# Early row maxima of a two-layer FNet and MQA kernel: one at a time, behind any matmul slot where a build-time estimate has a PSUM bank free

## The chip, the cores and the metric

One NeuronCore of one Trainium2 chip runs the whole program. The metric is the device time of one execution in microseconds (us). The kernel before was timed three times; the number to be predicted is the same time for the changed kernel.

The engines are named as the profile names them: PE is TensorE's matrix array (PEld its weight loads), DVE VectorE, ACT ScalarE, POOL GpSimd, SP SyncE, which issues most DMAs. PE writes its results into PSUM banks, from which DVE and ACT read them.

## The reference

Two layers, each an FNet mixing sublayer (A) and a multi-query attention sublayer (B), with S = 2048 rows, D = 512, H = 32 heads of 16:

```python
def _A_ref(x, ...):                       # FNet: y = Real(DFT_seq(DFT_hidden(x)))
    a = einsum("bsd,ed->bse", x, dft_hid_re); b = einsum("bsd,ed->bse", x, dft_hid_im)
    return einsum("ts,bse->bte", dft_seq_re, a) - einsum("ts,bse->bte", dft_seq_im, b)
def _B_ref(x, wq, wk, wv, wo):            # one k and one v for all 32 heads
    q = (x @ wq) ...; k = x @ wk; v = x @ wv
    scores = einsum("bhqd,bkd->bhqk", q, k) * Dh ** -0.5
    return einsum("bhqk,bkd->bhqd", softmax(scores), v) ... @ wo
x = A_x
for _ in range(2):
    x = x + _A_ref(_layernorm(x), ...)
    x = x + _B_ref(_layernorm(x), ...)
```

Products that need float32 accuracy are made of three products of a high and a low part (`mm3`: high times high, high times low, low times high).

## The kernel before

**Phases.** Each layer has a phase A (`phase_a`) and a phase B (`phase_b`). Phase A is a loop over 128 steps n. The steps stand in four blocks tb of 32 (one block makes 512 output rows); in a block the first 16 steps add up the real part and the next 16 the imaginary part of z = (layer-normed x) times the DFT matrix of the sequence, one 128-row chunk of the sum per step. After step 31, 63 and 95 (and in two parts at the end) the block's four row tiles are multiplied by the DFT matrix of the hidden axis (y), added to x, normalised, transposed (`tr_tile`), and multiplied into k and v (`kv`) and q (`q_mm`) during the first eleven steps of the next block; q is stored in DRAM (`qd`) and loaded back for one row tile i at a time (`qT_load`, 1 MB, a DMA on SP's queue). Phase B has 512 steps of scores, exponentials (ACT) and products with v.

**Row halves.** From step ROWS = 48 on, z (`z_rows`, L691) and y (`y_rows`, L494) use matmuls on half of PE's rows: each slot is a pair, one matmul on rows 0 to 63 (g = 0) and one on rows 64 to 127 (g = 1), which run side by side. A z step is 12 such pairs.

**Early maxima.** Softmax needs the maximum of each query row over the 2048 keys, for 16 row tiles i, 16 head pairs pr and two heads g. Each maximum is over four key quarters kb of 512. One matmul of a row half gives the 128 x 512 scores of one head and one quarter in one PSUM bank, and DVE reduces them (L381). Phase B makes most of them, up to three per step (`more_max`); a part is made early, in phase A from step 48 on. The table EARLY lists these: (i, quarter, slot for q, step of its `qT_load`, first time, last time). The times count 40 units per block, 32 for the steps and 8 for y. Quarter "f" means quarters 0 and 1 in one pass (`max_two`): two matmuls against the difference of the keys (L389, `kd`), their Relu on ACT (L394, tiles `rel` for g = 0 and `kraw` for g = 1), two matmuls against quarter 1, and one DVE instruction per g that adds and takes the maximum (L392). So one head pair of an "f" entry issues four matmuls in a row, and one of another entry two.

The order of all instructions is written out by this code at build time, and each engine runs its own in that order. Between z's pairs the early maxima stand at fixed places: `phase_a` spreads the 16 head pairs of an entry evenly between its two times, on quarters of a step (`inner`). They use three PSUM banks tagged "y", and one tagged "z"; the transposes also use "z", and `kv` and `q_mm` use "y". A matmul into a bank waits until DVE or ACT has read what the bank held, and since PE takes its matmuls in order, what stands behind it waits too.

Per layer EARLY has 8 entries of 32 plain maxima (256 matmuls) and 5 "f" entries of 64 matmuls (320), 576 in all.

Of the kernel before, what the change touches and what calls it, by code (L numbers as in the profile page):

```python
# [47 lines left out]
def fnet_mqa_kernel(ctx: ExitStack, tc: tile.TileContext, x_in, ct, dt_, wq, wkv, wo, out):  # L48
# [139 lines left out]
    def make_layer(L, src, mid, dst, last):  # L188
# [23 lines left out]
        def c_split(n):  # L212
            if n < 128:
                hls[n] = hl_tiles()
                split_sb(raws[n // 2][:, n % 2, :], *hls[n], None if L == 0 and n < 20 else nc.gpsimd)
# [36 lines left out]
        def tr_tile(t, x, xth, xtl, raw=None):  # L252
            pt = bank("z")
            for k in range(NK):
                nc.tensor.transpose(pt[:, k * P:(k + 1) * P], x[:, k * P:(k + 1) * P], ident)
            v = [ap.rearrange("p (a b) -> p a b", a=NK) for ap in (pt, raw or pt)]
            if raw:
                split_act(v[0], xth, xtl, v[1])
            else:
                split_ps(v[0], xth, xtl)  # L260

        def kv(t0, n, xth, xtl, vt=None, now=True):
            pk = bank("y")[:, :n * P]
            for k in range(NK):
# [11 lines left out]
        def kv_lo(t0, n):  # L276
            cs = slice(t0 * P, (t0 + n) * P)
# [4 lines left out]
        def k_diff(tb):  # L282
            if tb == 0:
# [17 lines left out]
        def q_mm(tb, g, xth, xtl):  # L301
            wh, wl = st["wqh", g]
            pq = bank("y")
            for k in range(NK):
# [63 lines left out]
        def partial(i):  # L368
            if i not in o.mxp:
                o.mxp[i] = sb.tile([P, NPAIR, 2, 4 if i else 5], F32, name=f"mxp{i % 4}")  # L370
                for e, (i_, kb, *_) in enumerate(KEPT):
                    for k in (0, 1) if kb == "f" else (kb,):
                        if i == i_:
                            nc.gpsimd.tensor_copy(o.mxp[i][:, :, :, k], st["mxe"][:, e])
# [8 lines left out]
        def max_two(i, pr, to):  # L383
            rows = [sb.tile([P, 512], F32, name=m) for m in ("rel", "kraw")]
            for k, c in ((st["kd"], 0), (kz, 512)):
                pm = [bank("z" if c and g else "y") for g in range(2)]
                for g in range(2):
                    gs = slice(64 * g, 64 * g + KR)
                    nc.tensor.matmul(pm[g], o.qT[i][gs, pr, :], k[gs, c:c + 512], start=True, stop=True)  # L389
                for g in range(2):  # L390
                    if c:
                        nc.vector.tensor_tensor_reduce(rows[g], pm[g], rows[g], 1.0, -3.0e38, ALU.add, ALU.max, to[:, g:g + 1])  # L392
                    else:
                        nc.scalar.activation(rows[g], pm[g], AF.Relu)  # L394

        def max_early(e, pr, at):
            i, kb = EARLY[e][:2]
            free = at < 80
            if "mxe" not in st:
                st["mxe"] = sb.tile([P, len(KEPT), NPAIR, 2], F32, name="mxe")  # L400
            if kb == "f":
                max_two(i, pr, st["mxe"][:, KEPT.index(EARLY[e]), pr] if i else partial(0)[:, pr, :, 0])
                if i == 0 and pr == NPAIR - 1:
                    nc.gpsimd.tensor_copy(partial(0)[:, :, :, 1], partial(0)[:, :, :, 0])
                return
            for g in range(2):
                to = st["mxe"][:, KEPT.index(EARLY[e]), pr, g:g + 1] if i else partial(0)[:, pr, g, kb:kb + 1]
                max_of(i, pr, g, kb * 512, 512, to, "z" if pr % 2 and g and free else "y")
# [66 lines left out]
        def y_out(t, y, x1):  # L475
            nc.vector.tensor_add(x1, y, x1)  # L476
# [6 lines left out]
        def y_rows(tb, pairs, zh, zl, x1, after):  # L483
            ys = [pair() for _ in pairs]
            at = 0
            for h in range(2):
                for w, y in zip(pairs, ys):
                    for cc, k in [(c, k) for c in range(2) for k in range(NK)][::1 - 2 * h]:
                        for u in (0, 1, 2)[::1 - 2 * h]:
                            a, b = ((zh, dh), (zh, dl), (zl, dh))[u]  # L490
                            for g in range(2):
# [3 lines left out]
                                                 start=(h, cc, k, u) == (0, 0, 0, 0), stop=(h, cc, k, u) == (1, 0, 0, 0))  # L495
                        for fn in after.get(at, ()):
# [78 lines left out]
        def prep_tasks(tb, x1):  # L575
# [15 lines left out]
            def ap(j):  # L591
                return lambda: ln_apply(x1[j], x1[j], 4 * tb + j)
# [21 lines left out]
        def phase_a(extra):  # L614
# [22 lines left out]
            for e, (i, kb, k, n0, n1, n2) in enumerate(EARLY):  # L637
                if n0 is not None:
                    add(n0, lambda i=i, k=k: qT_load(i, k))
                for pr in range(NPAIR):  # L640
                    u = n1 + pr * (n2 - n1) / NPAIR
                    at = divmod(int(4 * u), 4)
                    b, n = divmod(at[0], 40)
                    at = (32 * b + n, at[1]) if n < 32 else ("y", b, 4 * (n - 32) + at[1])
                    inner.setdefault(at, []).append(lambda e=e, pr=pr, u=u: max_early(e, pr, u))
# [26 lines left out]
            def z_split(z, hi, lo, c, d, late=False):  # L672
                if d % 2 == 0:
                    return
                if c or late:
                    for e in (d - 1, d):
# [5 lines left out]
            def z_rows(z, odd, chunks, first, last, split):  # L682
                order = [(j, u) for j in range(len(chunks)) for u in range(3)]
                for q in range(NK):
                    for e, (j, u) in enumerate(order[::-1] if q > 1 else order):
                        s, ch, cl = chunks[j]
                        a, b = ((xnh, ch), (xnh, cl), (xnl, ch))[u]
                        for g in range(2):
# [3 lines left out]
                                             start=first and q < 2 and e == 0, stop=last and q > 1 and e == len(order) - 1)  # L692
                        if 2 * e + 2 == len(order):
# [7 lines left out]
            def z_split_half(z, h, d):  # L701
                for e in (d - 1, d):
# [31 lines left out]
            for n in range(128):  # L734
# [12 lines left out]
                if n in (26, 58, 90, 114):  # L747
                    for tt in range(4):
                        x1[tt] = half(tt)
                        nc.sync.dma_start(x1[tt], src[4 * tb + tt])  # L750
# [376 lines left out]
```

## Time and profile before

| what | value |
|---|---|
| three runs | 3713.89, 3715.13 (median), 3718.11 us |
| the profiled execution: its own time; span of its instructions | 3717.63 us; 3715.8 us |
| granted TensorE clock, mean | 0.989 |
| busy: PE, DVE, ACT, POOL | 3607.8, 2644.9, 2533.2, 889.4 us |
| layer 0: first row-half matmul of z; last of them before y of block 3 | 203.3 us; 639 us |
| layer 1: the same two | 2048.3 us; 2478.8 us |
| phase B's exponentials are set up (ACT table load) in layer 0; in layer 1 | 717.8 us; 2557.7 us |

How to read it: times in the rows of a profile are us from the start of the span, those of one instruction in ns in the views that group. Matmuls are pipelined, and a matmul that starts every 0.23 us is shown as 0.39 us long, so that "busy" PE overlaps itself; how fast PE works is read from the starts, not from the busy share. A bracket at a row's end is the idle time before it and what ended it. The two layers run the same phase A program, so a stretch of one can be laid beside the same stretch of the other.

### The profile page before, as it was taken

What the parts mean: (1) busy time and instruction counts of PE and PEld (TensorE: products, weight loads), DVE (VectorE), ACT (ScalarE), POOL (GpSimd) and SP (SyncE); (2) the same over time, 40 slices, a digit from 0 to 9 for tenths busy, and PEclk for the clock granted to TensorE, in tenths of its full rate; (3) what the DMA queues carried; (4) which work ended last, traced back from release to release, by engine and by line L of the source; (5) the groups of instructions that cost most, each with busy time, mean ns of one, the idle gap of its engine ahead of it and who ended that gap; (6) DMA issues with size and microseconds to landing.
All of it is one profiled execution on the core that took longest, in us unless ns stands there. A gap on an engine that the chain in (4) does not pass through costs nothing.

```text
span 3715.8 us, 64466 instructions
## 1 busy us (share of the span) xinstructions
PE 3607.8 (97%) x24672; PEld 1866.1 (50%) x24672; DVE 2644.9 (71%) x4845; ACT 2533.2 (68%) x3278; POOL 889.4 (24%) x1270
## 2 busy tenths in 40 slices
PE   8999999999999999999999989999999999999999
PEld 6776667633333333333378756675333333333333
DVE  6155665588888888888411756666888888888882
ACT  3223544388888888888933245344888888888888
POOL 5543232112212211221254323231111011011101
PEclk9999999999999999999999999999999999999999
DMA  6544223311111110110134342324111111001101
GB/s 189 155 138 129 79 91 111 111 42 36 48 33 36 40 32 24 33 47 25 41 125 118 126 137 69 107 82 120 36 45 35 36 37 47 24 22 47 35 22 27
DMA packets 224389, 254.56 MB, mean 69 GB/s; under 512 B 52368, under 2 KB 174288, under 8 KB 216912
## 3 DMA queue, kind: packets, MB, share of 16 engines
q1 hardware_dynamic: 210384, 233.12, 20.8%
q0 software_dynamic: 13696, 17.33, 1.8%
q8 instruction: 194, 3.18, 0.4%
q14 instruction: 115, 0.94, 0.1%
HBM read 184.02 MB, written 65.27 MB: 67 GB/s over the span
## 4 chain that ended last, share of the span: by engine, by line
PE 85%; DVE 5%; ACT 4%; issue 3%; DMA 2%; POOL 1%; SPq 0%; ACTq 0%; POOLq 0%; DVEq 0%
PE z L866 27%; PE x L852 18%; PE y L380 14%; PE x L691 9%; PE x L494 2%; PE y L87 2%; PE y L88 2%; PE y L89 2%; PE x L89 2%; PE x L87 2%; PE x L88 2%; DVE mxe L381 1%; PE y L389 1%; ACT rel L394 1%; DVE kraw L392 1%
## 5 line engine op out<-in xcount | busy, mean ns | idle before, releaser
L855 ACT ACTIVATE slot<-x 128x1024 f32<-128x1024 f32 x1990 | 1938.3, 1025 | 297.1 <-PE x L852 282.6
L381 DVE TENSOR_REDUCE mxp<-y 128x1 f32<-128x512 f32 (+1 forms) x3040 | 1894.3, 678 | 219.5 <-PE y L380 205.4
L866 PE MATMUL z<-slot,v 128*32 128x512 f32 x8192 | 1098.9, 606 | 1.5 <-DVE lnv L977 0.7
L380 PE MATMUL y<-kz,slot 64*128 64x512 f32 (+1 forms) x2678 | 742.6, 401 | 27.8 <-DVE mxe L381 8.6
L852 PE MATMUL x<-slot,kz 64*128 64x512 f32 x2956 | 679.3, 453 | 6.6 <-DMA slot<-mt 4.3
L852 PEld LDWEIGHTS x<-slot,kz 64*128 64x128 f32 x2956 | 279.7, 185 | 749.5 <-ACT slot L855 674.7
L380 PEld LDWEIGHTS y<-kz,slot 64*128 64x128 f32 x2678 | 355.9, 188 | 100.0 <-DVE mxe L381 24.7
L79 POOL TENSOR_TENSOR cl<-craw,ch 128x512 fp32r<-128x512 f32 x236 | 302.3, 1298 | 334.9 <-ACT ch L78 271.2
L691 PE MATMUL x<-ch,xnh 64*128 64x512 f32 (+1 forms) x1536 | 338.6, 367 | 8.2 <-DVE row L476 6.2
L866 PEld LDWEIGHTS z<-slot,v 128*32 128x32 f32 x8192 | 164.4, 108 | 361.0 <-issue 330.6
L691 PE MATMUL x<-ch,xnl 64*128 64x512 f32 (+1 forms) x1536 | 337.9, 366 | 0.3
L381 DVE TENSOR_REDUCE mxe<-y 128x1 f32<-128x512 f32 x406 | 259.2, 684 | 110.9 <-PE y L380 86.0
L691 PE MATMUL x<-cl,xnh 64*128 64x512 f32 (+1 forms) x1536 | 336.2, 359 | 0.0
L448 POOL DMA_DIRECT2D slot<-mt x208 | 102.8, 502 | 615.9 <-PE y L380 559.4
L78 ACT CAST ch<-craw 128x512 fp32r<-128x512 f32 x256 | 152.6, 620 | 119.2 <-PE x L691 53.4
L392 DVE CUSTOM_DVE_ANT_0 rel<-y,rel 128x512 f32<-128x512 f32 x160 | 110.7, 692 | 171.4 <-ACT rel L394 133.2
L691 PEld LDWEIGHTS x<-ch,xnh 64*128 64x128 f32 x1536 | 192.8, 189 | 35.4 <-DVE row L476 7.7
L691 PEld LDWEIGHTS x<-cl,xnh 64*128 64x128 f32 x1536 | 200.4, 189 | 19.8
L907 POOL TENSOR_TENSOR row<-row,row 128x256 f32<-128x256 f32 x63 | 46.4, 737 | 680.0 <-DMA row<-rd 657.3
L691 PEld LDWEIGHTS x<-ch,xnl 64*128 64x128 f32 x1536 | 194.9, 189 | 23.2 <-issue 4.5
L394 ACT ACTIVATE rel<-y 128x512 f32<-128x512 f32 x160 | 95.4, 596 | 116.8 <-PE y L389 94.7
L87 PE MATMUL x<-ch,xnh 128*128 128x512 f32 x384 | 155.9, 406 | 14.7 <-ACT ch L78 11.5
(186 smaller groups left out, 3934.5 us busy)
## 6 DMA issues: line engine op xcount, KB each, us to landing
craw<-ct_in SPq DMA_DIRECT2D x112, 512.0 KB
slot<-qd SPq DMA_DIRECT2D x44, 1024.0 KB
qd<-row SPq DMA_DIRECT2D x144, 128.0 KB
od<-row SPq DMA_DIRECT2D x252, 64.0 KB
row<-wqd SPq DMA_DIRECT2D x48, 256.0 KB
row<-x_in SPq DMA_DIRECT2D x32, 256.0 KB
mid<-row POOLq DMA_DIRECT2D x32, 256.0 KB, 2.3
craw<-ct_in SPq DMA_DIRECT2D x32, 256.0 KB
```

What stands on the lines that cost most here:

```text
L78: nc.scalar.copy(hi, raw)
L79: (eng or nc.vector).tensor_sub(lo, raw, f(hi))
L87: nc.tensor.matmul(ps_, ah, bh, start=start, stop=False)
L88: nc.tensor.matmul(ps_, ah, bl, start=False, stop=False)
L89: nc.tensor.matmul(ps_, al, bh, start=False, stop=stop)
L380: nc.tensor.matmul(pm, o.qT[i][gs, pr, :], kz[gs, c0:c0 + n], start=True, stop=True)
L381: nc.vector.reduce_max(to, pm, axis=AX.X)
L392: nc.vector.tensor_tensor_reduce(rows[g], pm[g], rows[g], 1.0, -3.0e38, ALU.add, ALU.max, to[:, g:g + 1])
L691: nc.tensor.matmul(z[d], a[gs, s, d * P:(d + 1) * P], b[gs, :], start=first and q < 2 and e == 0, stop=last and q > 1 and e == len(order) - 1)
L852: nc.tensor.matmul(st["e"][:, g, :], kz[64 * g:64 * g + KR, c * P:(c + 1) * P], o.qT[i][64 * g:64 * g + KR, cp:cp + 4, :], start=True, sto ...
L855: nc.scalar.activation(ptiles[i, s_][:, 2 * w:2 * w + 2, :], st.pop("e"), AF.Exp, scale=DH ** -0.5)
L866: nc.tensor.matmul(a[32 * j:32 * j + 32, :], v1[:, c, :], pt[:, j, :], start=c == 0, stop=c == NT - 1)
```

## The change

1. The fixed places go. Every entry of EARLY becomes a list of single matmuls (`work`): head pair, part ("u" a plain maximum; "d" the difference and "b" quarter 1 of an "f" entry), g. After each pair of z (`z_rows`) and of y (`y_rows`) the code calls `pump`, which emits at most one of them: of the entries whose first step has come, the one with the earliest last step, if its next single is on the right row half and if the estimate has a bank free.
2. The estimate (`clk`) is kept while the program is written: `spend` adds fixed costs for the work that is emitted, `serve` gives DVE 0.6 and ACT 0.5 us for each item, and `held` notes until when a bank is taken, whichever of the four is free first. `flush` emits without regard to it what an entry still has left when its last step comes.
3. A single matmul on one row half shifts the halves by one slot: from there each pair of z and y is emitted with g = 1 first (`order`, `st["skew"]`), until the next single, so that the halves still take turns.
4. EARLY has other entries, steps (now counted in n) and loads. The "f" entry of row tile 0 becomes two plain ones, (2, 2) goes, and (1, 2) comes for 8 head pairs. Per layer that is 304 plain maxima and 4 "f" entries (256 matmuls), 560 in all; `units` gives phase B the other 16. There are as many `qT_load` as before, at steps 44, 44, 45, 64, 77, 77, 84, 96, 96, 101, 107 where they were at 44, 44, 50, 66, 66, 78, 78, 95, 97, 101, 107.
5. In phase B the shifts of row tile 14 are gathered in two halves of 8 head pairs, as those of tile 15 were, which adds 16 small DMAs per layer, 8 on SP's queue and 8 on POOL's.

```diff
 EARLY = [
-    (1, 0, 2, 44, 56, 63.5), (2, 0, 3, 44, 63.5, 70.9), (3, 0, 8, 50, 70.9, 86.5),
-    (0, "f", 0, 66, 88, 95), (1, 1, 1, 66, 87, 95), (3, 1, 8, None, 88.25, 112),
-    (4, "f", 2, 78, 95.5, 103), (5, "f", 3, 78, 103, 110.9), (6, "f", 8, 95, 115.5, 122.5),
-    (2, 1, 0, 97, 122.5, 128), (2, 2, 0, None, 128, 133.9), (7, "f", 2, 107, 136, 143), (0, 2, 8, 101, 134.5, 148.5),
+    (1, 0, 2, 44, 48, 63, 16), (2, 0, 3, 44, 48, 63, 16), (3, 0, 8, 45, 48, 66, 16), (0, 0, 0, 64, 66.5, 79, 16),
+    (0, 1, 0, None, 71.5, 79, 16), (3, 1, 8, None, 71.5, 84, 16), (4, "f", 2, 77, 79.5, 95, 16), (5, "f", 3, 77, 79.5, 95, 16),
+    (6, "f", 8, 84, 87, 128, 16), (2, 1, 0, 96, 98, 111, 16), (1, 1, 1, 96, 98, 111, 16), (1, 2, 1, None, 103.5, 111, 8),
+    (7, "f", 2, 107, 109.5, 119, 16), (0, 2, 8, 101, 103.5, 128, 16),
 ]
...
-        def max_two(i, pr, to):
...
-        def max_early(e, pr, at):
...
+        clk = {"pe": 0.0, "dve": 0.0, "act": 0.0, "y": [0.0] * 3, "z": 0.0}
+        def spend(pe=0.0, dve=0.0, act=0.0):
+            clk["pe"] += pe
+            for k, v in (("dve", dve), ("act", act)):
+                if v:
+                    clk[k] = max(clk[k], clk["pe"]) + v
+        def serve(eng, ready):
+            clk[eng] = max(clk[eng], ready) + (0.6 if eng == "dve" else 0.5)
+            return clk[eng] + 0.2
...
+        def pump(n, only=None):
+            for e in sorted((e for e in work if work[e] and EARLY[e][4] <= n), key=lambda e: EARLY[e][5]):
+                if only in (None, e) and work[e][0][2] == st["skew"] and issue(e, *work[e][0], only is not None):
+                    work[e].pop(0)
+                    st["skew"] ^= 1
+                    return True
+            return False
+        def issue(e, pr, part, g, force):
...
+            tag = "z" if clk["z"] <= clk["y"][0] else "y"
+            free = clk["z"] if tag == "z" else clk["y"][0]
+            if part == "b":
+                free = max(free, st["rel"][g][1] - 0.7)
+            elif part == "d" and g in st["rel"]:
+                return False
+            if free > clk["pe"] + 0.05 and not force:
+                return False
...
+            pm = bank(tag)
+            nc.tensor.matmul(pm, o.qT[i][gs, pr, :], k[gs, c0:c0 + 512], start=True, stop=True)
+            ready = max(clk["pe"], free) + 0.5
...
+                end = serve("dve", ready)
+            held(tag, end)
+            clk["pe"] += 0.116
+            return True
+        def flush(n):
+            for e in work:
+                while work[e] and EARLY[e][5] <= n:
+                    if not pump(n, e):
+                        assert any(pump(n, k) for k in work if work[k])
+                    clk["pe"] = max(clk["pe"], clk["dve"] - 1.0)
+        def order(*x):
+            return x[::-1] if st["skew"] else x
...
-                        for g in range(2):
+                        for g in order(0, 1):
                             d = ((0, 2, 1, 3), (1, 3, 0, 2))[g ^ odd][q]
...
+                        spend(pe=0.231 if len(chunks) == 2 else 0.116)
+                        pump(st["n"])
...
-                for at, j, p0, np_ in (..., (NSTEP - AHEAD, i + 1, 0, HALF if i == NT - 2 else NPAIR)):
-                    if j in (0, NT - 1) or j == i + 1 < NT:
+                for at, j, p0, np_ in (..., (NSTEP - AHEAD, i + 1, 0, HALF if i >= NT - 3 else NPAIR)):
+                    if j in (0, NT - 2, NT - 1) or j == i + 1 < NT:
```

What this does to the order on PE is seen at two places of layer 0. The first is step 72, just behind block 1's q products (L87 to L89). `slot` is a q tile, `kd` the difference of the keys, `x` a bank of z, `y` and `z` the four banks of the maxima; x2 is a pair. Before:

```order
L691 MATMUL x<-ch,xnh 128x512 x2
L691 MATMUL x<-cl,xnh 128x512 x2
L691 MATMUL x<-ch,xnl 128x512 x2
L389 MATMUL y<-kd,slot_2758 128x512 x2
L389 MATMUL y<-kz,slot_2758 128x512
L389 MATMUL z<-kz,slot_2758 128x512
L380 MATMUL y<-kz,slot_2760 128x512 x2
L691 MATMUL x<-ch,xnh 128x512 x2
L691 MATMUL x<-cl,xnh 128x512 x2
L691 MATMUL x<-ch,xnl 128x512 x2
```

And now, from the same pair of z:

```order
L749 MATMUL x<-ch,xnh 128x512 x2
L440 MATMUL y<-kz,slot_2703 128x512
L749 MATMUL x<-cl,xnh 128x512 x2
L440 MATMUL z<-kz,slot_2703 128x512
L749 MATMUL x<-ch,xnl 128x512 x2
L440 MATMUL y<-kz,slot_2703 128x512
L749 MATMUL x<-ch,xnh 128x512 x2
L440 MATMUL y<-kz,slot_2703 128x512
L749 MATMUL x<-cl,xnh 128x512 x2
L440 MATMUL y<-kz,slot_2703 128x512
L749 MATMUL x<-ch,xnl 128x512 x2
```

Six maxima in a row, over four banks, became singles with a pair of z between any two. Over steps 72 to 79 the program before has 112 matmuls of maxima, and the changed one 55.

The second place is the first transpose of block 1, at step 66 (`ident` is the identity it multiplies by, `row` the normalised x). Before:

```order
L380 MATMUL y<-kz,slot_1791 128x512 x2
L691 MATMUL x<-ch,xnh 128x512 x2
L691 MATMUL x<-cl,xnh 128x512 x2
L691 MATMUL x<-ch,xnl 128x512 x2
L255 MATMUL z<-ident,row_2097 128x128 x4
```

And now:

```order
L749 MATMUL x<-cl,xnh 128x512 x2
L440 MATMUL y<-kz,slot_2703 128x512
L749 MATMUL x<-ch,xnl 128x512 x2
L440 MATMUL y<-kz,slot_2703 128x512
L749 MATMUL x<-ch,xnh 128x512 x2
L440 MATMUL y<-kz,slot_2703 128x512
L749 MATMUL x<-cl,xnh 128x512 x2
L440 MATMUL z<-kz,slot_2703 128x512
L749 MATMUL x<-ch,xnl 128x512 x2
L258 MATMUL z<-ident,row_2145 128x128 x4
```

The bank z, which no maximum had used for a long time there, is now taken by one a single pair ahead of the transposes.

More of the change, by code (lines that the diff above doesn't have):

```diff
@@ L282, in k_diff @@
         def k_diff(tb):
+            spend(dve=0.7 * tb, act=0.6)
             if tb == 0:
@@ new lines, in held @@
+        def held(tag, until):
+            if tag == "y":
+                clk["y"] = clk["y"][1:] + [until]
+            else:
+                clk["z"] = until
+        work = {e: [(pr, part, g) for pr in range(ent[6]) for part in ("db" if ent[1] == "f" else "u") for g in range(2)]
+                for e, ent in enumerate(EARLY)}
+        st["skew"], st["rel"] = 0, {}
+        def pump(n, only=None):
[5 more added lines that the diff above has]
+            return False
@@ L406, in max_early @@
-            for g in range(2):
-                to = st["mxe"][:, KEPT.index(EARLY[e]), pr, g:g + 1] if i else partial(0)[:, pr, g, kb:kb + 1]
-                max_of(i, pr, g, kb * 512, 512, to, "z" if pr % 2 and g and free else "y")
+            at = 0 if kb == "f" else kb
+            to = st["mxe"][:, KEPT.index(EARLY[e]), pr, g:g + 1] if i else partial(0)[:, pr, g, at:at + 1]
+            gs = slice(64 * g, 64 * g + KR)
+            k, c0 = (st["kd"], 0) if part == "d" else (kz, 512 if part == "b" else 512 * kb)
```

77 lines of the change are left out of this document (42 added, 35 removed).

## The prediction

> **What bounds the kernel now.** I read the page first (engines, chain), then the busy time by stretch, the groups of PE, its waits, and the timeline of two stretches.
>
> ```profile
> PE 3607.8 (97%) x24672; PEld 1866.1 (50%) x24672; DVE 2644.9 (71%) x4845; ACT 2533.2 (68%) x3278; POOL 889.4 (24%) x1270
> PE 85%; DVE 5%; ACT 4%; issue 3%; DMA 2%; POOL 1%; SPq 0%; ACTq 0%; POOLq 0%; DVEq 0%
> ```
>
> PE is the bound: it carries 85% of the chain that ended last. But a busy PE need not work at its pace. The change touches phase A between the first row-half matmul and y of block 3, a stretch that I call S: 203.3 to 639 us in layer 0, 2048.3 to 2478.8 us in layer 1. Busy time by stretch (us; then PE, PEld, DVE, ACT, POOL with counts, granted clock, DMA share, GB/s):
>
> ```profile
> 203.30:639.00 435.70, 409.56 (x3031) 301.90 (x3031) 280.18 (x610) 185.58 (x387) 140.51 (x123) 0.96 0.33 107
> 2048.30:2478.80 430.50, 402.39 (x3031) 295.52 (x3031) 280.24 (x610) 185.68 (x387) 140.50 (x123) 0.99 0.33 108
> 220.00:280.00 60.00, 59.78 (x518) 48.24 (x516) 42.34 (x69) 14.37 (x33) 18.96 (x17) 1.00 0.23 78
> 320.00:360.00 40.00, 34.49 (x163) 21.75 (x163) 21.51 (x51) 14.85 (x31) 10.01 (x8) 0.87 0.47 120
> 360.00:400.00 40.00, 35.53 (x202) 22.58 (x200) 27.11 (x65) 20.57 (x41) 12.30 (x11) 0.87 0.31 103
> ```
>
> In the quiet 60 us PE does 518 row-half matmuls, 0.116 us each, with early maxima among them. From 320 to 400 us it does less than half as many per us, at a granted clock of 0.87. The groups of PE in layer 0's S give its work:
>
> ```profile
> L691 PE MATMUL x<-ch,xnh 64*128 64x512 f32 x512 | 128.1, 411 | 4.1 <-DVE row L476 3.1 <-ACT row L82 1.0
> L380 PE MATMUL y<-kz,slot 64*128 64x512 f32 x225 | 73.3, 434 | 9.0 <-DVE mxe L381 4.3 <-ACT rel L394 4.1
> L389 PE MATMUL y<-kd,slot 64*128 64x512 f32 x160 | 55.8, 440 | 7.5 <-DVE mxe L381 4.4 <-ACT rel L394 2.4 <-DVE mxp L381 0.8
> L494 PE MATMUL x<-slot,slot 64*128 64x512 f32 x384 | 51.4, 398 | 0.7 <-ACT row L82 0.7
> L389 PE MATMUL z<-kz,slot 64*128 64x512 f32 x80 | 39.3, 492 | 1.3
> L389 PE MATMUL y<-kz,slot 64*128 64x512 f32 x80 | 37.3, 467 | 3.7 <-DVE mxe L392 1.2 <-ACT rel L394 1.0
> L691 PE MATMUL x<-ch,xnh 64*128 64x256 f32 x128 | 23.8, 293 | 0.2 <-ACT row L82 0.2
> L380 PE MATMUL z<-kz,slot 64*128 64x512 f32 x21 | 8.2, 390 | 0.0
> ```
>
> L691 stands there three times alike (its three products). Row halves of 512 columns: 3 x 512 + 225 + 160 + 384 + 80 + 80 + 21 = 2486, at 0.116 us 288.4 us. Of 256 columns: 3 x 128 = 384 at half that, 22.3. On the whole array: 3031 less these are 161, of which 40 are small transposes (about 4 us, an estimate) and 121 take two slots, 0.232 us, 28.1. In all 343 us. So S loses 435.7 - 343 = 92.7 us in layer 0 and 87.5 in layer 1: 180 us where no slot of PE is filled.
>
> Idle PE in layer 0's S, by what it waited for (us, times, longest):
>
> ```profile
> PE y L389 <- DVE mxe L381: 4.4, 12, 0.6
> PE y L380 <- DVE mxe L381: 4.3, 6, 1.1
> PE y L380 <- ACT rel L394: 4.1, 6, 1.6
> PE y L389 <- ACT rel L394: 3.3, 2, 2.4
> PE x L691 <- DVE row L476: 3.1, 2, 1.7
> PE y L389 <- DVE mxe L392: 1.2, 1, 1.2
> PE y L389 <- DVE mxp L381: 0.8, 3, 0.3
> ```
>
> The six rows on maxima are 18.1 us; the rest of the 92.7 is hidden by the drawn-out lengths of matmuls, or is a lower pace. One place shows both (start, length, what, idle before):
>
> ```profile
> 321.64 0.98 PE L380 MATMUL y<-kz,slot 64*128 64x512 f32 x2 [1.51 <-ACT rel L394]
> 325.66 1.05 PE L691 MATMUL x<-cl,xnh 64*128 64x512 f32 x2
> 326.09 1.05 PE L691 MATMUL x<-ch,xnl 64*128 64x512 f32 x2
> 332.57 0.39 PE L89 MATMUL y<-slot,row 128*128 128x512 f32 x1
> 332.89 0.51 PE L691 MATMUL x<-ch,xnl 64*128 64x512 f32 x2
> 333.23 0.39 PE L691 MATMUL x<-cl,xnh 64*128 64x512 f32 x2
> 333.46 0.40 PE L691 MATMUL x<-ch,xnh 64*128 64x512 f32 x2
> ```
>
> A burst of four maxima fills all banks, the next waits 1.51 us for ACT, and then pairs start every 0.43 us (325.66 to 326.09) where 0.23 is usual (333.23 to 333.46). The Trainium skill ("TensorE: Matmul & The Clock Gate", "Why this matters for your kernels") has the clock fall after gaps above some 3 us; by it none of these waits would cost clock. The trace says otherwise, 0.87 with no wait over 2.4 us. By the page the clock's share, (1 - 0.96) x 435.7 + 0.01 x 430.5 = 22 us, would stay, and my sum would be 22 us less of a gain.
>
> **The change, part by part.**
>
> *Singles for bursts.* What a bank costs:
>
> ```profile
> 337.34 2.48 DVE L381 TENSOR_REDUCE mxe<-y 128x1 f32<-128x512 f32 x4
> L381 DVE TENSOR_REDUCE mxp<-y 128x1 f32<-128x512 f32 x2976 | 1870.8, 684 | 210.8 <-PE y L380 198.5
> ```
>
> Four reductions in 2.48 us with a last one of 0.68: one per 0.60, which is what the estimate charges DVE. A bank is back 0.4 (matmul) + 0.68 us after its matmul at the least; the estimate takes 0.5 + 0.6 + 0.2 = 1.3. So it errs to the safe side, and PE's true pace (0.232 a pair against 0.231) adds slack. I take the waits of maxima on maxima as gone. DVE covers them: S has 280 us of DVE work in 436, and will have (304 - 256) x 0.6 - 32 x 0.69 = 7 us more in a shorter S, about 287 of 370. If that cover fails, each late reduction costs PE its lateness.
>
> *What stays in S, per layer.* Passing from row halves to the whole array and back costs 0.2 us behind (332.57 to 333.23 is 0.66 for two steps of 0.23) and, an estimate, as much ahead, for 8 transposes, 2 kv, 2 of v, 8 q: 20 x 0.4 = 8. Then the 3.1 us of L476, and 1.7 on the splits of L82 in the groups above. 13 in all.
>
> *What is late next.* (a) Transposes behind a single in bank z: by the order five of the eight in S, 0.35 to 0.47 us of slots behind it. Each waits 1.08 - 0.35 = 0.7 at the least, and 1.8 more with three reductions queued: 3.5 to 12.5, with the others (0.8 to 2.3 us behind) up to 17. I take 6, near the low end, since a stall lets DVE drain. (b) kv and q in y banks used 1.3 to 2.8 us earlier: 0 to 9, I take 2. (c) DVE stands still ahead of each block's first `ln_apply`, with maxima queued behind it now:
>
> ```profile
> L183 DVE TENSOR_SCALAR row<-row,mv,rs 128x512 f32<-128x512 f32 x48 | 38.2, 812 | 12.4 <-POOL rs L152 9.8 <-DMA mid<-row 2.5
> ```
>
> 9.8 us over six blocks is 1.6 each; two blocks in S: 0 to 3.2, I take 2. (d) `flush` puts nine and five maxima in a row at steps 95 and 119: each at up to 0.4 us over its slot, 3 (0 to 6). (e) Maxima queued on DVE ahead of y's additions: 0 to 4, 2. (f) The q loads stand 2 to 4 steps ahead of their first use, where it was 1.5 to 13; on SP's queue those of steps 64, 84 and 96 pass a chunk load or two, which are needed six steps later, and SP still stands at slots 0 and 1 until y has read them:
>
> ```profile
> 2043.21 0.81 SPq L419 DMA_DIRECT2D slot<-qd  x2
> 2049.87 0.50 PE L380 MATMUL y<-kz,slot 64*128 64x512 f32 x2 [0.64 <-DMA slot<-qd]
> ```
>
> Landed 6.6 us after issue; two steps are 2 x 24 x 0.116 = 5.6 us, 6.4 with singles. 0 to 5, I take 1. (The 0.64 is the one wait of S on such a load; a lead of 1.5 steps showed none.) Together 13 + 16 = 29 us lost per layer, bounds 16.5 and 57.
>
> *Fewer singles.* 16 less per layer in S: 16 x 0.116 = 1.9 us. S becomes 343 - 1.9 + 29 = 370.1; saved 65.6 + 60.4 = 126.
>
> *Phase B takes them.* A usual stretch and the last one, without maxima (PE's products with v, eight records per step):
>
> ```profile
> 1082.40:1153.90 71.50, 34.10 (x256) 5.05 (x256) 1.00 0.14 39
> 1802.80:1866.00 63.20, 34.32 (x252) 6.13 (x248) 1.00 0.18 52
> ```
>
> 2.234 us a step against 63.2 / 31.5 = 2.006: 0.076 per maximum, 16 x 2 of them 2.4 us (bounds 0 and 32 x 0.2 = 6). The 16 DMAs per layer have six steps until they are needed: 0. POOL makes one copy of maxima less: 0.
>
> Sum: 126 - 2.4 = 123.6 us off the profiled execution's 3717.6, 3594. The median lies 2.5 below that execution: **3592 us**. With 16.5 or 57 us lost per layer it is 3567 or 3648.
>
> **Rivals.**
>
> *Slower: a lone matmul breaks the pairs.* If a single took a whole slot and left a half empty behind it, 3 x 0.116 instead of 0.116, 1120 singles would cost 1120 x 0.232 = 260 us: 3852. It decides from 123.6 / 1120 = 0.11 us per single. Against it, a place where a wait left the halves shifted by one:
>
> ```profile
> 519.18 0.39 PE L691 MATMUL x<-cl,xnh 64*128 64x512 f32 x1
> 519.19 0.39 PE L691 MATMUL x<-ch,xnh 64*128 64x512 f32 x1
> 519.41 0.40 PE L691 MATMUL x<-ch,xnl 64*128 64x512 f32 x1
> 519.42 0.39 PE L691 MATMUL x<-cl,xnh 64*128 64x512 f32 x1
> ```
>
> Two of different pairs per 0.23 us. 5 in 100.
>
> *Small waits keep the clock down.* If all of S ran at 0.87, as 320 to 400 us did, 0.13 x 400 = 52 us per layer would be lost again: 123.6 - 104 = 20 saved, 3695. For it: a single now comes just when a bank should be free, so that a late one makes PE wait a little each time; against it, the quiet 60 us, where DVE did 69 instructions and the clock was 1.00. 6 in 100. The Trainium skill (the page named above, "A second HAM failure mode: psum-queue depth-cycling") describes it.
>
> *Only recorded idle comes back.* The 18.1 us per layer, and the terms of 1.9 and 1.2: 2 x 18.8 = 37.6, 3677.5. For it: in layer 1's S the clock was 0.99 and the loss the same, so the loss is mostly not clock. Against it, the pace of 320 to 400 us. 6 in 100.
>
> *It doesn't do what it says.* The order shows the singles spread; only waits in a and b as large as those removed would leave no change: 3 in 100.
>
> **How the numbers follow.** 80 in 100 for the forecast with its bounds, 3567 to 3648; I widen to **3562 to 3655** for the reading of slots, which leaves the rivals out, 20 in 100. A change within 0.2% (7.4 us) is about what a measurement of this kernel can't tell from none. Faster 0.8 + 0.06 + 0.06 = 0.92, same 0.03, slower 0.05.
>
> **What would show it.** Right: S near 370 us in both layers; 320 to 400 us with over 300 matmuls per 40 us and clock 1.00; idle on maxima under 6 us per layer; a new row of transposes waiting for a reduction in z. Phase B as long as before within 2 us per layer. Wrong: pairs of z starting over 0.25 us apart beside singles, a clock under 0.95 in S, or transposes, kv and q waiting over 20 us per layer.

## The result, and the profile after

The changed kernel takes 3598.1 us (median of 4 runs, 3593.0 to 3599.3) against 3715.7 for the kernel before on the same chip: a ratio of 0.968, 95% interval 0.9664 to 0.9697, 118 us less. Forecast were 3592 and a range of 3562 to 3655. The profiled execution took 3599.3 us, 1.9 more than its span.

From its page, the engines and the shares of the chain that ended last:

```profile
PE 3513.1 (98%) x24672; PEld 1891.4 (53%) x24672; DVE 2685.1 (75%) x4853; ACT 2504.9 (70%) x3204; POOL 897.0 (25%) x1284
PE 87%; DVE 4%; issue 3%; ACT 3%; DMA 2%; POOL 1%; SPq 0%; ACTq 0%; POOLq 0%; DVEq 0%
```

PE is busy 94.7 us less and more of the span: its matmuls, as many as before, are shorter. Busy time by stretch (us; then PE, PEld, DVE, ACT, POOL, with counts, clock, DMA share, GB/s): S of both layers, from the first row-half matmul to y of block 3, then the two stretches that stood at a clock of 0.87.

```profile
202.70:576.30 373.60, 358.40 (x3010) 312.47 (x3010) 287.36 (x588) 170.76 (x354) 140.45 (x122) 1.00 0.38 125
1984.90:2358.30 373.40, 357.89 (x3010) 309.68 (x3010) 287.18 (x588) 170.69 (x354) 140.48 (x122) 1.00 0.38 124
320.00:360.00 40.00, 38.80 (x269) 31.14 (x268) 30.46 (x51) 11.03 (x24) 13.97 (x12) 1.00 0.63 170
360.00:400.00 40.00, 39.77 (x339) 36.97 (x336) 32.80 (x83) 29.41 (x61) 18.11 (x16) 1.00 0.35 134
```

S lost 62.1 us in layer 0 and 57.1 in layer 1. The 40 us from 320 and from 360 held 163 and 202 matmuls; now they hold 269 and 339, at full clock. DVE has 7 us more work than before (287 us for 280), in 374 us where it had 436.

What PE still waits for in layer 0's S (us, times, longest):

```profile
PE z L258 <- DVE mxp L454: 3.4, 3, 2.0
PE z L258 <- DVE mxe L454: 2.7, 3, 1.4
PE x L749 <- ACT row L82: 2.6, 4, 1.6
PE x L749 <- DVE row L537: 1.8, 2, 0.9
PE y L87 <- DVE mxe L454: 1.4, 3, 0.5
PE y L87 <- DVE mxp L454: 0.9, 2, 0.5
PE z L440 <- DMA slot<-qd: 0.4, 1, 0.4
PE y L440 <- ACT rel L444: 0.2, 1, 0.2
PE y L440 <- DVE mxe L449: 0.2, 1, 0.2
```

The line numbers have moved: an early maximum is L440 (it was L380 and L389), its reduction L454 or L449 (L381, L392), its Relu L444 (L394), z is L749 (L691), a transpose L258, the additions of y are L537 (L476). Maxima that wait for maxima or for their Relu: 0.4 us, in place of 18.1. New is the first pair of rows, transposes behind a single that still holds bank z.

### The profile page after: what moved, and what is told of

It reads as the page before. It is cut to its first block, busy times and chain, and to the rows that moved or that the text cites. A ratio compares the mean times of both kernels' runs of the same rounds, so it can differ in the third digit from the quotient of the medians.

```text
span 3597.4 us, 64452 instructions
## 1 busy us (share of the span) xinstructions
PE 3513.1 (98%) x24672; PEld 1891.4 (53%) x24672; DVE 2685.1 (75%) x4853; ACT 2504.9 (70%) x3204; POOL 897.0 (25%) x1284
## 4 chain that ended last, share of the span: by engine, by line
PE 87%; DVE 4%; issue 3%; ACT 3%; DMA 2%; POOL 1%; SPq 0%; ACTq 0%; POOLq 0%; DVEq 0%
PE z L930 28%; PE x L916 19%; PE y L389 13%; PE x L749 10%; PE y L87 2%; PE x L555 2%; PE y L440 2%; PE y L89 2%; PE y L88 2%; PE x L89 1%; PE x L87 1%; PE x L88 1%; DVE mxe L454 1%; DVE mxp L454 1%; PE z L440 1%
## 5 line engine op out<-in xcount | busy, mean ns | idle before, releaser
L390 DVE TENSOR_REDUCE mxp<-y 128x1 f32<-128x512 f32 (+1 forms) x3008 | 1872.7, 678 | 200.7 <-PE y L389 182.0
L389 PE MATMUL y<-kz,slot 64*128 64x512 f32 (+1 forms) x2240 | 598.3, 394 | 5.4 <-DVE kz L286 3.0
L749 PE MATMUL x<-cl,xnh 64*128 64x512 f32 (+1 forms) x1536 | 354.5, 354 | 0.0
L749 PE MATMUL x<-ch,xnh 64*128 64x512 f32 (+1 forms) x1536 | 342.5, 359 | 9.0 <-ACT row L82 5.3
L749 PE MATMUL x<-ch,xnl 64*128 64x512 f32 (+1 forms) x1536 | 347.5, 359 | 0.0
L389 PEld LDWEIGHTS y<-kz,slot 64*128 64x128 f32 x2240 | 288.2, 187 | 29.8 <-DVE mxp L390 11.4
L440 PE MATMUL y<-kz,slot 64*128 64x512 f32 x602 | 233.5, 399 | 2.0 <-DVE kraw L296 1.0
L749 PEld LDWEIGHTS x<-ch,xnh 64*128 64x128 f32 x1536 | 213.8, 185 | 27.7 <-ACT row L82 9.1
L749 PEld LDWEIGHTS x<-cl,xnh 64*128 64x128 f32 x1536 | 220.8, 185 | 7.6
L749 PEld LDWEIGHTS x<-ch,xnl 64*128 64x128 f32 x1536 | 216.3, 185 | 12.8 <-issue 4.8
L454 DVE TENSOR_REDUCE mxe<-y 128x1 f32<-128x512 f32 x310 | 194.9, 678 | 14.2 <-PE y L440 14.0
L87 PE MATMUL x<-ch,xnh 128*128 128x512 f32 x384 | 155.6, 405 | 14.2 <-ACT ch L78 10.8
L88 PE MATMUL x<-cl,xnh 128*128 128x512 f32 x384 | 154.3, 402 | 3.4 <-POOL cl L79 2.8
```

What stands on the lines that cost most here:

```text
L87: nc.tensor.matmul(ps_, ah, bh, start=start, stop=False)
L88: nc.tensor.matmul(ps_, ah, bl, start=False, stop=False)
L389: nc.tensor.matmul(pm, o.qT[i][gs, pr, :], kz[gs, c0:c0 + n], start=True, stop=True)
L390: nc.vector.reduce_max(to, pm, axis=AX.X)
L440: nc.tensor.matmul(pm, o.qT[i][gs, pr, :], k[gs, c0:c0 + 512], start=True, stop=True)
L454: nc.vector.reduce_max(to, pm, axis=AX.X)
```

## The experiments

All kernels but one are edits of the changed kernel; their times are medians, to be read against its 3598.1. Where steps are timed, it is from the first matmul of z of the one to that of the other in layer 0; steps differ in length, since other work stands between.

**Two at a time.** In `pump`, and in `issue` the question is put for two banks:

```diff
                     work[e].pop(0)
-                    st["skew"] ^= 1
+                    issue(e, *work[e].pop(0), True)
...
-            if free > clk["pe"] + 0.05 and not force:
+            both = sorted([clk["z"], *clk["y"]])[1]
+            if max(free, both - 0.116) > clk["pe"] + 0.05 and not force:
```

> The changed kernel, but early maxima go out two at a time (both row halves), when the estimate has two banks free, and the halves never shift. By the kernel's own estimate the waits on full banks then sum to 22 us per layer, most of them in the runs that are forced at the end of a window, where they sum to 5 in the changed kernel. Theory (what counts is that no maximum meets a full bank): +10 to +17 us per layer, 3618 to 3632. Rival (it is the single, shifting one that counts): most of the 119 us comes back, 3680 to 3715.

3630.1 us (ratio to the kernel before 0.9772, 0.9757 to 0.9787). S is 388.8 and 390.3 us, 16 longer per layer, as the theory has it at its upper end. Pairs with the question put keep 73% of the gain, and the step from two to one is worth 32 us of 118. Where those 32 us lie is seen by stretch, in layer 0: steps 48 to 88 of this kernel, then steps 88 to 104 of the changed kernel and of this one:

```profile
202.60:396.00 193.40, 184.14 (x1473) 158.52 (x1475) 147.69 (x263) 67.41 (x148) 76.66 (x66) 1.00 0.40 130
396.60:501.40 104.80, 99.75 (x792) 82.74 (x788) 79.80 (x193) 61.39 (x122) 33.42 (x32) 1.00 0.27 97
396.00:510.60 114.60, 106.51 (x799) 83.23 (x795) 79.39 (x200) 63.23 (x126) 33.38 (x32) 0.97 0.26 88
```

The changed kernel takes 193.9 us for steps 48 to 88, so two at a time cost nothing there (1.5 us in layer 1). Steps 88 to 104 are 9.8 us longer at a lower clock, and the rest of S 5.8. Windows end in these two stretches, at steps 95 and 119, and what is left then is forced. That fits the expectation, which had most of the waits there: the pairs cost mainly by what they leave over for the end of a window.

**The order of the pairs.** `order(*x)` returns `x` always:

> The changed kernel, but each pair is always written row half 0 first; the singles still take turns between the halves. Theory (matmuls of the two halves start in their order as each half comes free, so the turns of the singles alone keep both halves filled, and an order of the pair costs at most a half slot at each return from the whole array): 3596 to 3603. Rival (the order of the pairs must follow the shift): a half slot of 0.116 us lost per two singles, 560 x 0.116 = 65 us, 3663.

3596.5 us, S 374.3 and 373.6: no difference, so the shifting of the halves by the code is not needed. The next kernel turns each pair the wrong way (`return x if st["skew"] else x[::-1]`):

> The changed kernel with the order of each pair turned the wrong way, so that a single is always followed, on its own half, by the first matmul of the next pair. Theory (a half left empty is a loss on the bound engine): one half slot lost per single, 1120 x 0.116 = 130 us, less some waits on banks that the slower pace takes away: 3705 to 3728. Rival (PE has slack beside the singles, or fills the half from further behind): 3598 to 3610.

3596.4 us, S 373.8 and 373.7. The theory fell: a half that the program's order leaves without work costs nothing. Its timeline (start, length, what):

```profile
220.18 0.47 PE L749 MATMUL x<-ch,xnh 64*128 64x512 f32 x2
220.41 0.39 PE L440 MATMUL z<-kz,slot 64*128 64x512 f32 x1
220.50 0.54 PE L749 MATMUL x<-cl,xnh 64*128 64x512 f32 x2
220.73 0.54 PE L749 MATMUL x<-ch,xnl 64*128 64x512 f32 x2
220.96 0.39 PE L440 MATMUL y<-kz,slot 64*128 64x512 f32 x1
```

The single at 220.41 is on row half 0, and the program has the pair's matmul of half 0 behind it, then the one of half 1. If they started in that order, the first of the pair would have to wait 0.23 us for its half. A matmul starts 0.09 us behind the single, and from one single to the next are 0.55 us, less than five half slots (0.58). So it is half 1's that starts first. The trace says so too where a pair raises a semaphore: the program has the update on the later matmul of the second pair (220.73), and the record that carries it is the earlier one.

**No estimate.** The question is taken out, so that a single follows each slot while its window is open:

```diff
-            if free > clk["pe"] + 0.05 and not force:
-                return False
+            clk["pe"] = max(clk["pe"], free)
```

> The changed kernel without the question whether a bank is free: from the opening of its window on, a single goes out behind every slot until its entry is done. By the estimate PE then waits for banks 90 us per layer (306 waits of some 0.25 to 0.3), where the changed kernel has 5. Theory (full banks are what cost before): +70 to +90 us per layer, with a lower clock where the waits stand: 3735 to 3780, slower than the kernel before. Rival (singles between pairs are enough, no estimate is needed): 3598 to 3615.

3746.3 us: slower than before the change (ratio 1.0084, 1.0069 to 1.0099). S is 451.4 and 450.1 us. Its first 58.8 us (eight steps, which took 28.9 in the changed kernel) by stretch, and some of its matmuls there:

```profile
202.10:260.90 58.80, 56.52 (x287) 29.44 (x287) 55.92 (x94) 9.30 (x22) 13.50 (x11) 0.97 0.25 91
224.52 0.73 PE L748 MATMUL x<-ch,xnl 64*128 64x512 f32 x2
225.11 0.50 PE L439 MATMUL y<-kz,slot 64*128 64x512 f32 x1
225.12 0.72 PE L748 MATMUL x<-ch,xnl 64*128 64x512 f32 x2
225.71 0.50 PE L439 MATMUL z<-kz,slot 64*128 64x512 f32 x1
225.72 0.73 PE L748 MATMUL x<-cl,xnh 64*128 64x512 f32 x2
```

A single and a pair every 0.60 us, where three half slots are 0.35: PE runs at the pace of DVE, which is busy 55.9 of 58.8 us. No idle time on a bank is recorded; PE shows as busy for 56.5, with lengths of 0.50 for 0.39. The loss of the kernel before from 320 to 400 us was not of this kind alone: DVE was busy there for 21.5 and 27.1 of 40 us, and the clock was 0.87. Singles that go out as early as their window lets them are no gain, then; the question for a free bank makes them one.

**Even spacing, no estimate.** The question is taken out here too, and the k-th of N singles goes out no earlier than k/N of its window:

```diff
+                tot = EARLY[e][6] * (4 if EARLY[e][1] == "f" else 2)
+                due = EARLY[e][4] + (EARLY[e][5] - EARLY[e][4]) * (1 - len(work[e]) / tot)
+                if only is None and n < due:
+                    continue
...
-            if free > clk["pe"] + 0.05 and not force:
-                return False
+            clk["pe"] = max(clk["pe"], free)
```

> The changed kernel with singles set out evenly over their windows (the k-th of N no earlier than k/N of the window) and sent without asking whether a bank is free; one window is closed at step 100 so that its slot can be loaded again. By the estimate 39 us of waits per layer (128 late singles) where the changed kernel has 5. Theory (full banks cost; spacing alone does not see the other work of VectorE, nor two windows that are open at once): +20 to +34 us per layer, 3638 to 3666. Rival (even spacing of singles is enough): 3593 to 3606.

3666.5 us, S 405.8 and 405.5: the theory, at the very top of its range. The row shows one of the places that even spacing does not see, a clock of 0.81 with 106 matmuls in 20 us:

```profile
420.00:440.00 20.00, 18.95 (x106) 11.69 (x104) 16.35 (x48) 15.11 (x29) 2.56 (x2) 0.81 0.16 54
```

**The old windows.** The changed planner with the table of before:

```diff
-    (1, 0, 2, 44, 48, 63, 16), (2, 0, 3, 44, 48, 63, 16), (3, 0, 8, 45, 48, 66, 16), (0, 0, 0, 64, 66.5, 79, 16),
-    (0, 1, 0, None, 71.5, 79, 16), (3, 1, 8, None, 71.5, 84, 16), (4, "f", 2, 77, 79.5, 95, 16), (5, "f", 3, 77, 79.5, 95, 16),
...
+    (1, 0, 2, 44, 48, 56, 16), (2, 0, 3, 44, 55.5, 63, 16), (3, 0, 8, 50, 62.9, 71, 16), (0, "f", 0, 66, 72, 79, 16),
+    (1, 1, 1, 66, 71, 79, 16), (3, 1, 8, None, 72.25, 95, 16), (4, "f", 2, 78, 79.5, 87, 16), (5, "f", 3, 78, 87, 95, 16),
...
```

> The changed planner (singles, the estimate) with the windows of the table before, written as steps: 576 singles per layer, in the order and the windows in which the kernel before had them, each done as early in its window as the estimate lets it. By the estimate 17 us of waits per layer, 89 singles forced at ends of windows, against 5 and 13. Theory (single and estimate do it, the wider windows only keep them from being forced): +10 to +15 us per layer, less 1 for the 32 maxima that phase B no longer has: 3616 to 3630. Rival (the new windows carry half of the gain or more): 3657 or more.

3659.7 us: the rival, and a miss. The expectation had counted how late singles are when they go out, and not the time that `flush` itself adds to the estimate (its last line) at the end of a window. S of layer 0, its steps 72 to 80, and 20 us in them:

```profile
204.30:611.00 406.70, 389.60 (x3034) 318.67 (x3034) 288.06 (x613) 188.96 (x388) 140.82 (x123) 0.95 0.35 115
322.30:382.10 59.80, 58.52 (x327) 42.65 (x326) 40.71 (x96) 29.91 (x60) 15.97 (x14) 0.86 0.51 150
360.00:380.00 20.00, 19.21 (x50) 10.68 (x51) 19.83 (x39) 2.81 (x5) 0.24 (x1) 0.59 0.08 27
```

Here 50 matmuls stand in 20 us at a clock of 0.59, with DVE busy throughout: 96 maxima are due by step 79 from windows that open at 71 and 72. The changed kernel takes 39.7 us for these steps. To see whether this jam is all, 32 of its maxima alone were moved to where the new table has them (`(1, 1, 1, 96, 98, 111, 16)`):

> The changed planner with the old windows, but for one: the 32 maxima that the old table has at steps 71 to 79 beside 64 others go to steps 98 to 111, as in the new table. With the old windows steps 72 to 80 took 60 us per layer against 40 in the changed kernel, with PE at clock 0.59 for 20 us. Theory (what the new table adds is the end of that one jam, where more maxima are due than VectorE can reduce): 15 to 19 us less per layer than with the old windows, 3622 to 3630. Rival (the short windows cost everywhere, or the jam moves to where the 32 now are): 3645 to 3660.

3635.2 us, S 392.7 and 393.1: between the two. Steps 72 to 80 fell from 59.8 to 44.2 us, but steps 104 to 112, which have the 32 now, rose from 38.4 to 47.8, and steps 80 to 96 stayed 13 us above the changed kernel (107.2 to 94.2). The jam is the largest single part of what the old windows cost (15.6 of 33 us in layer 0), and part of it moves with the maxima.

**Bank z kept free.** In `issue`:

```diff
-            tag = "z" if clk["z"] <= clk["y"][0] else "y"
+            at = st.get("n", 0)
+            soon = at >= 64 and 1.5 <= at % 32 < 4.9
+            tag = "z" if clk["z"] <= clk["y"][0] and not soon else "y"
```

> The changed kernel, but singles keep out of bank z from 1.5 to 4.9 steps into blocks 2 and 3, where six of the transposes stand that need it. Takes away the term (a) of the prediction. Theory (the transposes wait because a reduction holds z): 6 us of recorded waits per layer go, and a short stretch of half clock behind the longest: 12 to 16 us in all, 3582 to 3586. Rival (VectorE is late there anyway, so that the wait passes to the rows that it has to normalise or to a y bank): 3594 to 3600.

3589.1 us (3587.0 to 3591.6, all below the changed kernel's runs; ratio to before 0.9664, 0.9651 to 0.9677), S 369.8 and 369.5. By the ratios, whose intervals overlap, that is 6 us less than the changed kernel. The head of its waits in layer 0's S:

```profile
PE x L751 <- ACT row L82: 2.6, 4, 1.6
PE z L442 <- ACT v L306: 2.1, 1, 2.1
PE x L751 <- DVE row L539: 1.8, 2, 0.9
PE y L87 <- DVE mxe L456: 1.6, 4, 0.5
PE y L87 <- DVE mxp L456: 1.1, 3, 0.5
```

No transpose waits for a reduction in z any more: 6.1 us of waits are gone per layer. S is 3.8 and 3.9 us shorter by it; a single in z behind the transposes of v now waits 2.1 us where it waited 0.3, and the rows of kv grew by 0.4. Both theories hold in part. That wait was taken on next, by 5.9 to 7.2 added to `soon`, with one window opened a step earlier:

> The kernel that keeps singles out of bank z ahead of the transposes, with two more edits: z also kept free from 5.9 to 7.2 steps into those blocks, where the small transposes of v use it (in that kernel a single behind them waited 2.1 us for ScalarE), and one window opened a step earlier (65.5 for 66.5), by which 15 singles are forced instead of 14, thus no gain by that. Theory: 2.1 us less per layer, 3583 to 3586. Rival (the wait goes to the next bank): 3587 to 3591, no change against that kernel.

3592.7 us: no gain, with S at 368.3 and 368.1 but the stretch from there to the first score at 86.3 us in layer 0, where the changed kernel has 82.4: a transpose in that stretch now waits 1.8 us for a reduction in z. The wait went on to the next place. The version that keeps z free for the transposes is the fastest of all that ran.

**One side.** After the orders had made no difference, singles that do not take turns: `work[e]` of the plain entries is sorted by row half, and `pump` no longer asks for `st["skew"]`:

> The changed kernel, but the singles do not take turns between the row halves: of the 304 plain ones per layer up to 16 in a row go to row half 0, then 16 to half 1 (the others still take turns). Written because neither order of the pairs mattered. Theory (each half has its own row of matmuls and runs ahead of the other for a few of them at most, so that a half without a single stands empty beside it): 0.116 us per plain single, 2 x 304 x 0.116 = 70 us, 3640 to 3670. Rival (the pace is one 64-row matmul per 0.116 us whatever the half, or the halves may drift apart without limit): 3595 to 3605.

3643.6 us, within the theory's range, but by two causes, neither at the theory's price, as the rows below show. And with two in a row on a half (sorted by `(u[0] // 2, u[2])`):

> The kernel of singles that do not take turns, but with two in a row on each row half (0, 0, 1, 1) for the plain singles in place of sixteen. With sixteen it took 3643.6, 0.072 us per plain single more. Theory (a half runs ahead of the other by a few matmuls, so that a drift of two is made good): 3596 to 3606. Rival (the matmul behind a second single on one half has to wait each time, half of the plain singles at 0.116 us: 2 x 152 x 0.116 = 35 us): 3625 to 3640.

3615.6 us, outside both. Steps 48 to 88, then 88 to 96, first of the changed kernel, then with sixteen, then with two in a row:

```profile
202.70:396.60 193.90, 187.19 (x1483) 165.97 (x1485) 149.56 (x271) 70.18 (x152) 76.64 (x66) 0.99 0.40 130
396.60:460.00 63.40, 62.00 (x520) 54.99 (x518) 48.13 (x143) 49.22 (x96) 16.43 (x14) 1.00 0.17 59
203.90:408.90 205.00, 200.47 (x1482) 165.29 (x1484) 157.27 (x269) 70.05 (x151) 76.61 (x66) 1.00 0.38 123
408.90:478.70 69.80, 68.34 (x520) 53.24 (x518) 50.53 (x146) 49.91 (x97) 16.42 (x14) 0.93 0.16 54
202.90:400.20 197.30, 189.23 (x1483) 164.82 (x1485) 151.15 (x269) 70.09 (x151) 76.53 (x66) 0.98 0.40 130
400.20:469.30 69.10, 66.96 (x520) 52.66 (x518) 50.42 (x146) 49.87 (x97) 16.39 (x14) 0.95 0.16 54
```

Steps 88 to 96 are 6 us longer in both, at a lower clock: without the turns 25 maxima are forced at step 95 instead of 9, some 0.4 us for each of the 16 more. Neither expectation had that. In steps 48 to 88 sixteen in a row cost 11.1 us for 192 plain singles, 0.058 each, half of the 0.116; two in a row cost 3.4 in layer 0, but there PE waited 1.9 us for a load of q at the start, with pairs 0.43 us apart behind it. In layer 1, without that wait, these steps took 193.0 us against 193.9: no cost. So two in a row on a half cost nothing, and sixteen do. The reading is that a drift of two between the halves mends itself and one of sixteen does not; where between the limit lies stays open.

**Phase B.** It came out shorter where a longer one was forecast, which is an effect in the kernel before. One number of that kernel is changed:

```diff
-                        if s_ == 4:
+                        if s_ == (2 if j == 13 else 4):
                             o.loaded.add(j)
```

> The kernel before, with one number changed: row tile 13 counts as loaded from step 2 of row tile 11 on, not from step 4. Theory for the term of phase B that came out with the other sign (the kernel before runs out of units of loaded row tiles at step 354, sends fewer maxima for two steps and then four per step, and loses 3.9 us per layer by it; the changed kernel has 16 units more ahead of them and does not run out): -4 to -8 us in all against the kernel before, 3707 to 3711, and the stretch of steps 352 to 368 as long as in the changed kernel. Rival (the difference there has another cause): 3713 to 3717, no change.

3708.1 us against 3713.4 (ratio 0.9985, 0.9976 to 0.9994): the theory. Steps 352 to 368 of layer 0, of the kernel before, of the changed one, and of this one:

```profile
1513.10:1554.20 41.10, 39.27 (x256) 15.47 (x252) 31.38 (x53) 31.11 (x34) 2.45 (x4) 1.00 0.17 52
1451.10:1488.40 37.30, 37.30 (x258) 14.59 (x254) 31.48 (x53) 31.17 (x34) 2.47 (x4) 1.00 0.18 56
1508.30:1545.70 37.40, 37.40 (x258) 14.64 (x254) 31.57 (x53) 31.27 (x34) 2.46 (x4) 1.00 0.18 56
```

The same work in 41.1 us, and in 37.3 and 37.4. The kernel before has no unit of a loaded row tile at step 354, sends fewer maxima for two steps and then four a step, which meet full banks: PE waits 1.6 us for reductions in this stretch, and not at all in the changed kernel. The 16 units that the change puts ahead of them move that place behind the load.

## Why the prediction was right, and where not

**The mechanism** was named right: slots of PE that full banks left empty. No estimate brings the whole loss back and more (451 us of S, above the 436 of the kernel before), with singles, turns and windows as they are. What the prediction did not split is the gain: put back one at a time, two in place of one cost 32 us, the old table of windows 62, the missing estimate 68 with even spacing and 148 without. They overlap and do not add up. The new steps of the q loads and the halved shifts of row tile 14 were not put back; steps 368 to 480 of phase B, where those shifts stand, take 248.6 us in layer 0 of both kernels.

**S** was to be 370.1 us and is 373.6 and 373.4. With the 20 singles less that are counted below, slots are 343 - 2.3 = 340.7, so the loss is 32.9 and 32.7, where 29 was taken. Recorded idle is 15 of it, and the half clock shown further down (3.4 us long) some 1.7; the rest stands in no row. Transposes behind a single, (a): 6.1 us in the rows above, 6 taken. kv and q, (b): 2.3, 2 taken. q loads, (f): 0.4, and 0.8 in layer 1, 1 taken. The splits of L82, among "what stays", were 1.9 in the prediction's rows (1.7 in its sum) and are 3.4 (2.6 above, 0.8 on y): the term that was too small among those that a row shows. (c), (d) and (e) have no row of their own: the additions of y wait 1.8 where 3.1 + 2 was taken, and `ln_apply` shows in no row. For (d) the runs without turns give a price, 0.4 us for each single forced at step 95; at that price the 13 forced in the changed kernel would be 5 us, where 3 was taken. That is an estimate, since no run took those 13 away. Passing to the whole array and back (8) was not tested.

**Fewer singles** in S: right in kind, with 20 less for 16. S holds 546 early maxima per layer where it held 566; of the kernel's 560 the last 14 stand behind y of block 3, of the 576 before it was 10.

**Phase B** had the wrong sign. The end without maxima, of the kernel before and of the changed one:

```profile
1802.80:1866.10 63.30, 62.58 (x401) 23.65 (x397) 10.78 (x26) 59.61 (x93) 14.62 (x30) 1.00 0.18 52
1737.20:1802.70 65.50, 64.34 (x418) 23.93 (x414) 21.08 (x42) 60.04 (x88) 14.70 (x30) 1.00 0.17 50
```

16 more reductions cost 2.2 us, 0.14 each, where 0.076 was taken from a mean over steps: 4.4 in both layers against 2.4. But 3.8 us per layer came back at steps 352 to 368. The step that failed is the bound "0 and 6": it looked at what a maximum costs, not at what moving the queue of units by 16 does to a place where the queue runs dry. With both, layer 1 before S and phase B of layer 0 together came out 2.0 us shorter and phase B of layer 1 0.9, 2.9 where +2.4 was forecast.

**A term left out**: from y of block 3 to the first score it takes 1.3 us more in layer 0 and 3.0 in layer 1. It was taken as untouched, and no run tries it. Four more early maxima stand there, 0.5 us of slots. Layer 1 differs from layer 0 in the clock, which is 1.00 in layer 0; here are the whole stretch in layer 1 and 3.3 us of it:

```profile
2358.30:2442.50 84.20, 75.60 (x769) 64.44 (x769) 43.68 (x94) 19.88 (x53) 18.55 (x31) 0.97 0.20 61
2421.10:2424.40 3.30, 3.30 (x16) 2.92 (x15) 0.69 (x1) 1.30 (x3) 0.00 (x0) 0.50 0.47 99
```

At a clock of 0.50 these 3.3 us lose about 1.7, which is the difference between the layers. What else the 1.3 us are stays open.

The sum from the spans, 3715.8 to 3597.4: -119.2 in S, +4.3 there, -2.9 in phase B, -0.6 at the start, -118.4. Forecast were -123.6: S is 6.8 short, the term left out 4.3, phase B 5.3 the other way. That the total came within 6 us is luck in part, since the wrong sign of phase B made good half of the other two.

**The signs to look for.** Clock 1.00: right. Idle on maxima under 6 us: 0.4, right, with transposes and kv 8.8. The new row of transposes: right. "Over 300 matmuls per 40 us": 339 and 269, wrong for the first stretch, which has four q projections on the whole array, whose 48 matmuls take two half slots each. Phase B within 2 us per layer: right.

**The rivals.** A lone matmul does not break the pairs: not even the wrong order does (3596.4), and the price that would decide, 0.11 us per single, is not reached by sixteen on one side (0.058). Small waits do not keep the clock down: it is 1.00 with 15 us of recorded idle in S. More came back than recorded idle: 119 us, not 37.

The one stretch at half pace that is left in layer 0's S shows how small a wait does it:

```profile
294.26 0.86 PE L258 MATMUL z<-ident,row 128*128 128x128 f32 x4 [2.00 <-DVE mxp L454]
296.49 0.63 PE L749 MATMUL x<-ch,xnh 64*128 64x512 f32 x2
296.92 0.63 PE L749 MATMUL x<-ch,xnl 64*128 64x512 f32 x2
298.57 0.40 PE L749 MATMUL x<-cl,xnh 64*128 64x512 f32 x2
298.80 0.40 PE L749 MATMUL x<-ch,xnh 64*128 64x512 f32 x2
```

After 2.00 us of idle, pairs start 0.43 us apart, and 0.23 from 298.57 on. The Trainium skill ("TensorE: Matmul & The Clock Gate", "Why this matters for your kernels") puts the limit at gaps above some 3 us; this trace does not agree, as the prediction had it. By that rule the clock's share would have stayed, some 22 us by the prediction's estimate; it came back, but for the stretch above and one like it in layer 1.

## What to carry to other kernels

When a busy engine runs below its pace without recorded idle, compare the work in slots with the time, stretch by stretch: here 180 us of loss stood against 37 of recorded waits on the cause. Filler work pays only where its buffer is free and its consumer has time: spread it by an account of both, and look at the end of each window, since what is forced there undoes it. Before costing units added to a queue, find where the queue runs dry; moving it can be worth more than the units.

## What the runs showed of the hardware

The two row halves of TensorE do not start in the program's order. With the order turned against them the time stayed at 3596.4 us, matmuls of one half start 0.23 us apart each on its own, and the half that is free goes ahead. The description of the kernel before has PE take its matmuls in order; between the two halves that is not so. The same page of the Trainium skill ("TensorE: Matmul & The Clock Gate", "The mechanism") has matmuls start and end strictly in order; by that, 1120 singles would have lost 0.116 us each, an estimate of 130 us, and none of it was seen. Two singles in a row on one half cost nothing (193.0 us against 193.9 for steps 48 to 88 of layer 1), sixteen cost 0.058 us each.

A bound by DVE can leave PE busy for 96% (56.5 of 58.8 us), with no wait for a bank in any row: it is seen in the spacing of starts, 0.60 us for 0.35, and in DVE at 95%.
